# Fetching V of an attention block by one 1 MB DMA per step in place of two of 0.5 MB

## Chip, cores, metric

The kernel runs on one core of one Trainium2 chip. The metric is the device time of one execution in microseconds. Where two kernels are compared, they ran on the same chip in alternating rounds; the ratio is the mean time of one kernel's runs over that of the other's of the same rounds, so it is not quite the ratio of the medians that are quoted. A bracket after a ratio is its 95% interval. In the profiles PE is TensorE (PEld its weight loads), DVE is VectorE, ACT is ScalarE, POOL is GpSimd, and SP is SyncE, which here issues the DMAs.

## The reference

Two attention blocks with a cache of K and V, for 16 batches of 32 queries. A has 4 K/V heads shared by 32 query heads; B has 32 K/V heads of its own. The outputs are put side by side.

```python
# per block: x [16,32,1024], k_cache and v_cache [16,Hkv,1024,128], all bf16
q = (x @ wq).reshape(B, Sq, 32, 128).transpose(0, 2, 1, 3)
scores = einsum("bhqd,bhkd->bhqk", q, k) * 128 ** -0.5
o = einsum("bhqk,bhkd->bhqd", softmax(scores), v)
out = o.transpose(0, 2, 1, 3).reshape(B, Sq, 4096) @ wo
```

B's caches dominate the traffic: K and V of B are 128 MB (of 2^20 bytes) each.

## The kernel before

B is done in 128 steps. A step takes four heads of one batch: 1 MB of K and 1 MB of V. K has two slots in SBUF, V has three. A step of A runs beside each step of B.

```python
NVB_SLOTS = 3          # V of B
NKB_SLOTS = 2          # K of B
DMA_BW = 390e3         # what the scheduler believes of the DMA, bytes per us
SP_AHEAD = 1.5         # how far ahead of the DMA stream it lets SP issue, us

def st_dmaV(q):        # ... (the branch for B)
    sl = q.vslot
    for t_ in range(2):
        vsrc = pb["v"][q.b, q.h0 + 2 * t_:q.h0 + 2 * t_ + 2].rearrange("a (p c) d -> p a c d", c=NCH)
        pr.add("sp", lambda e, t_=t_, vsrc=vsrc: e.dma_start(VB_sb[:, sl, 2 * t_:2 * t_ + 2, :, :], vsrc),
               writes=[("VB", sl, t_)], dma_key=f"vb{sl}_{t_}", name="vb_dma", dur=2 * Sk * Dh * 2, ...)

# the value product of step q reads both halves
pr.add("pe", lambda e, c0=c0: e_pv(e, c0), reads=["PT", ("VB", kvs, 0), ("VB", kvs, 1)], writes=[BK_O], name="PVB", ...)
```

Nothing is issued in the order of these calls. Every operation is first put on a list with what it reads and writes and how long it should take. `list_schedule` then simulates all engines and the DMA stream, picks at each moment the ready operation with the longest way to the end, and so fixes the order of each engine's instructions. A DMA occupies the simulated stream for `dur / DMA_BW`:

```python
if op.dma_key is not None:
    free[op.eng] = st + 0.06
    xs = max(st + 0.06, dma_free[0])
    dma_free[0] = xs + op.dur / dma_bw
    op.t1 = dma_free[0] + dma_lat
# ...
seq = sorted(range(n), key=lambda k: (ops[order[k]].t0, k))     # the new order of the program
# ... in build():
pr = pr.list_schedule()
pr.finalize()                                                    # semaphores and waits
```

All DMAs go out on SP in the order of its program: a DMA that waits for its slot or its data holds all that stand behind it. The last additions of the output projection write a row block into one staging buffer, `ost`, from which an output DMA takes it. There are eight such blocks, and each has to leave before the next can be written.

## Time and profile before

| | before |
|---|---|
| time, median of the first 3 runs | 855.66 us (854.54 to 856.07) |
| span of the profiled run | 853.9 us |
| bytes moved, mean rate | 341.6 MB, 400 GB/s |

These lines are from the summary page of before: busy time per engine, the rate in 40 equal slices, the count of DMA packets, the share of 16 DMA engines' time that the SP queue's packets take, and for two kinds of DMA their count, size and median time from issue to landing.

```profile
PE 726.1 (85%) x12098; PEld 434.9 (51%) x12098; DVE 545.3 (64%) x1115; ACT 447.1 (52%) x981; POOL 67.9 (8%) x76
GB/s 353 395 411 400 412 405 409 413 410 377 407 406 405 416 411 412 410 401 415 409 409 411 410 412 406 413 410 414 413 401 411 397 410 413 414 411 411 412 385 158
DMA packets 126845, 341.59 MB, mean 400 GB/s; under 512 B 9984, under 2 KB 9984, under 8 KB 110336
q1 hardware_dynamic: 126720, 339.78, 100.7%
KB_sb<-in_B_k_cache_dram SPq DMA_DIRECT2D x128, 1024.0 KB, 8.9
VB_sb<-in_B_v_cache_dram SPq DMA_DIRECT2D x256, 512.0 KB, 10.1
```

The DMA stream is the bound: it is full from the first slices to the last but one, and no compute engine is. A 1 MB transfer lands 8.9 us after its issue because it queues behind others: at about 410 GB/s the megabyte itself is 2.6 us. The list of SP's own waits (who waited for whom: us in total, times, longest) shows that SP spends much of the span held by a buffer that isn't free yet, with that backlog in front of it:

```profile
SPq L784 <- DVE KBt_sb L819: 124.5, 36, 8.5
SPq L784 <- DVE stat L882: 100.9, 34, 5.9
SPq L791 <- POOL VAp_sb L793: 80.8, 28, 6.5
```

Line 784 issues K of B: it can go when DVE has done both transposes of the K that held the slot. When that slips, the backlog shrinks.

### The profile page before, as it was taken

Reading aid. Unit: us, or ns where it says so; the run is one execution under the profiler, and the core shown is the slowest. Engines: PE = TensorE matmul, PEld = TensorE weight load, DVE = VectorE, ACT = ScalarE, POOL = GpSimd, SP = SyncE. Lnnn points to the kernel's source line nnn. Section 1 sums busy time; section 2 is a strip of 40 time slices with the busy share of each in tenths; the row PEclk is TensorE's granted clock in tenths of the full one; section 3 lists DMA queues with packets and bytes.
Section 4 is the critical chain, followed back from the end, with each engine's and each line's share of the span. In section 5 each row is a group of like instructions: output and inputs, shape, how many; then the busy total and the mean of one; then the engine's idle time right before and its main releaser. Section 6 shows DMA issues by size and latency. Waiting matters only on the chain.

```text
span 853.9 us, 27413 instructions
## 1 busy us (share of the span) xinstructions
PE 726.1 (85%) x12098; PEld 434.9 (51%) x12098; DVE 545.3 (64%) x1115; ACT 447.1 (52%) x981; POOL 67.9 (8%) x76
## 2 busy tenths in 40 slices
PE   4999999789979897799997879887999867878885
PEld 2556655446545454455554445544555544545552
DVE  0755676567756677467774757675766755766673
ACT  2456666456645464445654445654565554556451
POOL 0000100100000000000000000000000000000000
PEclk9999999999999999999999999999999999999998
DMA  9999999999999999999999999999999999999994
GB/s 353 395 411 400 412 405 409 413 410 377 407 406 405 416 411 412 410 401 415 409 409 411 410 412 406 413 410 414 413 401 411 397 410 413 414 411 411 412 385 158
DMA packets 126845, 341.59 MB, mean 400 GB/s; under 512 B 9984, under 2 KB 9984, under 8 KB 110336
## 3 DMA queue, kind: packets, MB, share of 16 engines
q1 hardware_dynamic: 126720, 339.78, 100.7%
q8 instruction: 96, 1.57, 0.7%
q14 instruction: 29, 0.24, 0.1%
HBM read 337.64 MB, written 2.10 MB: 398 GB/s over the span
## 4 chain that ended last, share of the span: by engine, by line
DMA 49%; PE 29%; DVE 12%; SPq 5%; issue 3%; ACT 1%; POOL 0%; DVEq 0%; POOLq 0%
DMA KB_sb<-in_B_k_cache_dram 29%; DVE KBt_sb L819 10%; PE ps_pj L654 8%; PE ps_s L854 5%; DMA VB_sb<-in_B_v_cache_dram 5%; DMA KA_sb<-in_A_k_cache_dram 5%; PE ps_pj L708 4%; DMA VA_sb<-in_A_v_cache_dram 3%; PE ps_kt L912 3%; DMA wq_sb<-in_B_wq_dram 3%; PE ps_o L946 2%; SPq L799 2%; PE ps_pt L896 2%; PE ps_s L837 2%; DMA woB_sb<-in_B_wo_dram 1%
## 5 line engine op out<-in xcount | busy, mean ns | idle before, releaser
L819 DVE STREAM_TRANSPOSE KBt_sb<-KB_sb 128x1024 f32<-128x1024 f32 x256 | 306.2, 1226 | 75.8 <-DMA KB_sb<-in_B_k_cache_dram 67.8
L877 ACT ACTIVATE P_sb<-ps_s 128x512 bf16<-128x512 f32 x256 | 151.9, 599 | 88.3 <-PE ps_s L854 64.2
L869 ACT ACTIVATE PTA_sb<-ps_s 128x1024 bf16<-128x1024 f32 x128 | 131.3, 1026 | 89.8 <-PE ps_s L837 72.0
L854 PE MATMUL ps_s<-KBt_sb,QB_sb 32*32 32x512 bf16 x4096 | 144.4, 389 | 11.0 <-ACT P_sb L877 6.1
L584 ACT COPY PT_sb<-ps_pt 128x512 f32<-128x512 f32 x128 | 75.0, 586 | 122.3 <-PE ps_o L946 111.0
L654 PE MATMUL ps_pj<-xT_sb,wq_sb 128*128 128x512 bf16 x448 | 122.6, 392 | 10.7 <-DMA wq_sb<-in_B_wq_dram 3.7
L793 POOL COPY VAp_sb<-VA_sb 128x1024 bf16<-128x1024 bf16 x64 | 66.6, 1040 | 757.5 <-DMA VA_sb<-in_A_v_cache_dram 725.4
L946 PE MATMUL ps_o<-VB_sb,PT_sb 128*32 128x128 bf16 x4096 | 82.7, 223 | 35.4 <-DMA VB_sb<-in_B_v_cache_dram 21.2
L896 PE MATMUL ps_pt<-id,P_sb 128*128 128x128 f32 x512 | 99.2, 302 | 6.9 <-ACT P_sb L877 6.0
L946 PEld LDWEIGHTS ps_o<-VB_sb,PT_sb 128*32 128x32 bf16 x4096 | 61.2, 98 | 70.0 <-issue 66.1
L896 PEld LDWEIGHTS ps_pt<-id,P_sb 128*128 128x128 f32 x512 | 79.8, 206 | 27.3 <-ACT P_sb L877 9.6
L837 PE MATMUL ps_s<-QT_sb,KTA_sb 128*128 128x256 bf16 x512 | 83.1, 273 | 6.4 <-ACT PTA_sb L869 2.9
L912 PE MATMUL ps_kt<-VAp_sb,PTA_sb 128*128 128x129 bf16 x1024 | 77.8, 224 | 6.9 <-POOL VAp_sb L793 4.7
L854 PEld LDWEIGHTS ps_s<-KBt_sb,QB_sb 32*32 32x32 bf16 x4096 | 48.6, 89 | 65.7 <-issue 12.2
L962 DVE TENSOR_SCALAR OB_sb<-ps_o,rinv_all 128x128 bf16<-128x128 f32 x128 | 43.9, 343 | 59.4 <-PE ps_o L946 58.6
L912 PEld LDWEIGHTS ps_kt<-VAp_sb,PTA_sb 128*128 128x128 bf16 x1024 | 65.7, 99 | 31.6 <-POOL VAp_sb L793 14.0
L708 PE MATMUL ps_pj<-woB_sb,OTB_sb 128*128 128x512 bf16 x256 | 71.0, 384 | 10.0 <-DMA woB_sb<-in_B_wo_dram 3.8
L708 PE MATMUL ps_pj<-woA_sb,OTA_sb 128*128 128x512 bf16 x256 | 66.6, 385 | 7.9 <-DVE ost L724 3.5
L654 PEld LDWEIGHTS ps_pj<-xT_sb,wq_sb 128*128 128x128 bf16 x448 | 42.2, 109 | 45.9 <-DMA wq_sb<-in_B_wq_dram 6.3
L837 PEld LDWEIGHTS ps_s<-QT_sb,KTA_sb 128*128 128x128 bf16 x512 | 44.8, 98 | 30.4 <-ACT PTA_sb L869 7.1
L882 DVE TENSOR_TENSOR stat<-stat 64x1 f32<-64x1 f32 x256 | 41.9, 164 | 22.5 <-ACT P_sb L877 14.3
L721 DVE TENSOR_TENSOR acc<-acc,ps_pj 128x512 f32<-128x512 f32 x64 | 43.1, 674 | 20.4 <-PE ps_pj L708 19.1
(49 smaller groups left out, 504.8 us busy)
## 6 DMA issues: line engine op xcount, KB each, us to landing
KB_sb<-in_B_k_cache_dram SPq DMA_DIRECT2D x128, 1024.0 KB, 8.9
VB_sb<-in_B_v_cache_dram SPq DMA_DIRECT2D x256, 512.0 KB, 10.1
KA_sb<-in_A_k_cache_dram SPq DMA_DIRECT2D x64, 256.0 KB, 10.2
VA_sb<-in_A_v_cache_dram SPq DMA_DIRECT2D x64, 256.0 KB, 8.6
wq_sb<-in_B_wq_dram SPq DMA_DIRECT2D x16, 512.0 KB, 10.7
woB_sb<-in_B_wo_dram SPq DMA_DIRECT2D x32, 256.0 KB, 10.7
woA_sb<-in_A_wo_dram SPq DMA_DIRECT2D x32, 256.0 KB, 8.6
wq_sb<-in_A_wq_dram SPq DMA_DIRECT2D x12, 512.0 KB, 10.4
```

What stands on the lines that cost most here:

```text
L584: pr.add("act", lambda e: e.copy(dst_ap, src_ap), reads=reads, writes=writes, name=name + "@act", wtag=wtag, rtag=rtag)
L654: last = e.matmul(ps_pj[:, 0:NTOK], pick(src, j), xT_sb[:, pi, j, :], start=(j == 0), stop=(j == DJ - 1))
L708: last = e.matmul(ps_pj[:, 0:OUTW], OT[:, gp, hh, :], wo_[:, hh, oh * OUTW:(oh + 1) * OUTW], start=(hh == 0), stop=(hh == nh - 1))
L793: pr.add("pool", lambda g: g.tensor_copy(VAp_sb[:, sl, :, 0:Dh], VA_sb[:, :, :]), reads=["VA"], writes=[("VAp", sl)], name="VAp_cp", rtag= ...
L819: pr.add("dve", lambda e: e.transpose(KBt_sb[:, sl, t_, :].bitcast(F32).rearrange("p (s r i) -> p s r i", r=2, i=32), KB_sb[:, rs, t_, :]. ...
L837: last = e.matmul(ps_s[:, sbf, c2, i * 2 * P:(i + 1) * 2 * P], KTA_sb[:, sl, c * P:(c + 1) * P], qt, start=True, stop=True)
L854: last = e.matmul(ps_s[32 * cg:32 * cg + 32, sbf, g, :].rearrange("p (sh cl j) -> p sh cl j", sh=4, cl=4), lhsT, kt[32 * a:32 * a + 32, g, ...
L869: pr.add("act", lambda e: e.activation(dst, src, ACTF.Exp, scale=scale), writes=BK_S[sbf] + [("PTA", q.half)], name="expA", rtag={("Sv", s ...
L877: pr.add("act", lambda e, src=src, dst=dst, g=g: e.activation(dst, src, ACTF.Exp, scale=scale, accum_out=st[:, g:g + 1]), writes=[BK_S[sbf ...
L896: last = e.transpose(ps_pt32[:, m * P:(m + 1) * P], p32[:, m:Sk // 2:NPK], id32[:])
L912: last = e.matmul(ps_kt[:, qh * OA0:qh * OA0 + Dh + 1], PTA_sb[:, h, c, qh * P:(qh + 1) * P], VAp_sb[:, sl, 4 * h + c, 0:Dh + 1], start=(h ...
L946: last = e.matmul(ps_o[32 * a:32 * a + 32, 0:Dh], PT_pairs[:, c // 2, 32 * (a ^ (c // 4 * 2)):32 * (a ^ (c // 4 * 2)) + 32, c % 2], VB_sb[ ...
```

## The change

The intent is fewer, larger transfers: one DMA of 1 MB per step, one semaphore (the counter by which an engine learns that a transfer has landed), one wait. The diff is shortened at the dots.

```diff
-                for t_ in range(2):
-                    vsrc = pb["v"][q.b, q.h0 + 2 * t_:q.h0 + 2 * t_ + 2].rearrange("a (p c) d -> p a c d", c=NCH)
-                    pr.add("sp", lambda e, t_=t_, vsrc=vsrc: e.dma_start(VB_sb[:, sl, 2 * t_:2 * t_ + 2, :, :], vsrc), writes=[("VB", sl, t_)],
-                           dma_key=f"vb{sl}_{t_}", name="vb_dma", dur=2 * Sk * Dh * 2, wtag={("VB", sl, t_): q.kid})
+                vsrc = pb["v"][q.b, q.h0:q.h0 + 4].rearrange("a (p c) d -> p a c d", c=NCH)
+                pr.add("sp", lambda e: e.dma_start(VB_sb[:, sl, :, :, :], vsrc), writes=[("VB", sl)],
+                       dma_key=f"vb{sl}", name="vb_dma", dur=4 * Sk * Dh * 2, wtag={("VB", sl): q.kid})
...
-                pr.add("pe", ..., reads=["PT", ("VB", kvs, 0), ("VB", kvs, 1)], ...
+                pr.add("pe", ..., reads=["PT", ("VB", kvs)], ...
```

More of the change, by code (lines that the diff above doesn't have):

```diff
@@ L949, in st_pv @@
             for c0 in range(0, NCH, 2):
-                pr.add("pe", lambda e, c0=c0: e_pv(e, c0), reads=["PT", ("VB", kvs, 0), ("VB", kvs, 1)], writes=[BK_O], name="PVB",
-                       dur=0.116, tag="B%d" % q.t, rtag={"PT": q.qid, ("VB", kvs, 0): q.kid, ("VB", kvs, 1): q.kid}, wtag={"Ops": q.qid})
+                pr.add("pe", lambda e, c0=c0: e_pv(e, c0), reads=["PT", ("VB", kvs)], writes=[BK_O], name="PVB",
+                       dur=0.116, tag="B%d" % q.t, rtag={"PT": q.qid, ("VB", kvs): q.kid}, wtag={"Ops": q.qid})
         def st_recip(q):
```

## The prediction

> **What bounds the kernel now.** The DMA engines. The summary page gives 400 GB/s over the 853.9 us span; 34 of its 40 slices move 400 to 416 GB/s. Its queue table puts the SP queue's packets at 100.7% of 16 engines' time. TensorE is busy 85%, DVE 64%, ACT 52%. I also summed the issues and the packet records: between 20 and 830 us the bytes issued but not yet moved had a median of 2.6 MB and never fell under 0.3 MB. The engines always have a packet waiting, so time is bytes over rate, plus some 12 us of start and 15 us of drain.
>
> **What the change does.** V's bytes (128 MB), source runs (2 KB) and 65,536 data packets stay. There are 128 DMA instructions fewer (of 624) and 16 x 128 = 2,048 semaphore packets fewer (of 9,984, the "under 512 B" count). A 4-byte packet takes 9 ns in the records: 2,048 x 9 ns / 16 = 1.2 us goes away. A gap around each could add up to 1 us. Data packets keep their 84 ns per 2 KB (1st and 95th percentile alike).
>
> On SP the timeline shows 0.95 us for the two issues; one of twice the size should take 0.75 to 0.95 us. SP mostly waits (124.5 us on DVE's K transposes, by its list of waits) behind that backlog, so this is worth nothing. TensorE's value product read both halves already; its 21.2 us of waiting for V is off the critical path.
>
> The Trainium skill, "DMA: Bandwidth & Descriptors", section "Rules for kernel authors", asks for 1 MiB or more per DMA; its section "Bandwidth" rates single 1 MB transfers at 78% of peak. That promises a gain if transfers stand alone. Here they don't: the fixed cost hides under the backlog, and this mix of 0.25, 0.5 and 1 MB DMAs already streams at about 410 GB/s.
>
> **What moves.** The kernel orders its instructions by a list scheduler of its own, fed with each DMA's size. One entry in place of two reorders the SP queue and, through it, all engines. K of B can no longer slip between two halves of V. K has two slots; it lands 8.9 us after its issue (median), then come two transposes, 2.4 us: 11.3 us against two steps of 6.6 us (stream time / 128), about 2 us of slack; half a V is 1.3 us. Some backlog is lost, but it should not run dry. The end (last V issued at 831.3 us behind an output DMA, last instruction at 853.9) can shift a few us either way: the main spread.
>
> **Prediction.** 855.7 - 1.2 (semaphore packets) - up to 1 (gaps) + about 1 (coarser order) = 854.8 us; 8 in 10 within 850.5 to 860. Faster by over 2%: 0.01; within 2%: 0.96; slower by over 2%: 0.03.
>
> **What would show it.** Right: 496 issues, 7,936 packets under 512 B, data packets still 84 and 309 ns, slices still 400 to 416 GB/s, V's issue-to-landing 1 to 2 us above 10.1 us. Wrong: V packets slower; middle slices under 390 GB/s, or DVE waiting clearly more than 67.8 us for K (backlog ran dry); a tail 5 us longer or shorter.
>
> **What would make it wrong.** A reordered queue in which SP waits for a V or A slot with K behind it, so the stream starves each step; or four interleaved head streams in HBM running at another rate than two.

## The result

After took 859.69 us (median of 4 runs, 858.03 to 860.53) against 855.1 us for before (4 runs, 853.86 to 856.07). The ratio is 1.0051 [1.0035, 1.0068]: within 2% as forecast, and just inside the range, but the small effect has the opposite sign. I had expected to gain about 1 us; about 4 us were lost. That the time lies within the range is owed to the range's width. The same lines of the page of after:

```profile
PE 708.6 (83%) x11967; PEld 432.1 (50%) x12098; DVE 546.7 (64%) x1115; ACT 449.8 (52%) x981; POOL 67.9 (8%) x76
GB/s 342 387 406 389 412 411 409 410 415 406 407 408 409 409 410 400 412 414 399 407 399 412 411 411 416 392 409 415 405 413 413 407 404 411 415 412 411 409 373 108
DMA packets 124795, 341.56 MB, mean 398 GB/s; under 512 B 7936, under 2 KB 7936, under 8 KB 108288
q1 hardware_dynamic: 124672, 339.77, 100.3%
KB_sb<-in_B_k_cache_dram SPq DMA_DIRECT2D x128, 1024.0 KB, 9.0
VB_sb<-in_B_v_cache_dram SPq DMA_DIRECT2D x128, 1024.0 KB, 11.3
```

What was to be removed is removed: 128 issues, and 2,048 packets under 512 B. In the packet records the semaphore packets' time fell from 5.6 to 4.5 us per DMA engine. (PE's lower busy time comes with matmul records missing from the trace: 11,967 of 12,098.) The rest of the run looks much the same; the lowest slices are among the first four and the last two.

A view by windows says the same with less noise. Its columns are the window, its length, busy time and instruction count of PE, PEld, DVE, ACT and POOL, PE's clock, DMA share, and the rate in GB/s as the last number. First before, then after:

```profile
40.00:80.00 40.00, 39.16 (x498) 23.12 (x497) 21.23 (x46) 21.75 (x44) 3.13 (x3) 1.00 1.03 399
80.00:820.00 740.00, 638.77 (x10979) 385.12 (x10978) 490.96 (x1007) 403.45 (x892) 61.38 (x59) 0.98 1.03 409
```

```profile
40.00:80.00 40.00, 38.30 (x491) 23.37 (x498) 22.62 (x48) 21.61 (x43) 3.12 (x3) 1.00 1.01 384
80.00:820.00 740.00, 620.04 (x10853) 380.19 (x10965) 491.02 (x1005) 406.08 (x893) 60.79 (x59) 0.98 1.03 409
```

From 80 to 820 us both move 409 GB/s (a rounded figure: 1 GB/s more or less over 740 us would be 1.8 us). Between 40 and 80 us after moves 15 GB/s less, which is 0.6 MB, or 1.5 us of stream at 409 GB/s. From the packet records I took the time at which given amounts of data had been moved: after reached 26 MB 1.7 us later than before, needed 0.5 us less from there to 326 MB, 1.5 us more from 326 to 339 MB, and 2.0 us more from 339 MB to its end. That adds up to 4.7 of the 4.8 us between the two spans. In this pair of traces the loss is at the two ends. (One trace is one execution: five other traces with before's engine order reached 26 MB at 67.6 to 69.5 us, four others with after's at 68.5 to 70.6 us, so such a number scatters by about 2 us. The profiled execution of after, 860.53 us, was the slowest of its four.)

What goes on at the start can be read in the timelines (start, length, engine, line, operation, destination<-source, shape, count, and in brackets the idle time before and what ended it). Before, DVE and then SP:

```profile
46.45 2.37 DVE L819 STREAM_TRANSPOSE KBt_sb<-KB_sb 128x1024 f32<-128x1024 f32 x2 [0.36 <-DMA KB_sb<-in_B_k_cache_dram]
49.83 0.69 DVE L586 CAST QT_sb<-ps_pj 128x512 bf16<-128x512 f32 x1 [1.01 <-PE ps_pj L654]
...
48.85 0.33 SPq L784 DMA_DIRECT2D KB_sb<-in_B_k_cache_dram  x1
```

After, DVE and then SP:

```profile
47.31 1.25 DVE L818 STREAM_TRANSPOSE KBt_sb<-KB_sb 128x1024 f32<-128x1024 f32 x1 [1.69 <-DMA KB_sb<-in_B_k_cache_dram]
49.77 0.69 DVE L586 CAST QT_sb<-ps_pj 128x512 bf16<-128x512 f32 x1 [1.21 <-PE ps_pj L654]
...
51.64 1.25 DVE L818 STREAM_TRANSPOSE KBt_sb<-KB_sb 128x1024 f32<-128x1024 f32 x1
...
52.91 0.33 SPq L784 DMA_DIRECT2D KB_sb<-in_B_k_cache_dram  x1
```

Before does the two transposes of a K back to back, and SP issues the next K at 48.85 us. In after the scheduler put a copy of a projection between them. That copy waits for TensorE, more small work follows, and the second transpose only ends at 52.9 us. The next K goes out 4.1 us later, and V and the rest wait behind it on SP. This is a different order of DVE's instructions. No DMA has become slower.

That this late K costs the time is not shown, and finer windows speak against the simplest reading. First before, then after:

```profile
40.00:50.00 10.00, 9.69 (x123) 4.83 (x125) 5.76 (x14) 3.92 (x11) 1.05 (x1) 1.00 1.03 393
50.00:60.00 10.00, 9.91 (x147) 5.90 (x135) 6.51 (x12) 5.59 (x11) 0.28 (x1) 1.00 1.03 415
60.00:70.00 10.00, 10.00 (x140) 6.58 (x138) 6.27 (x14) 6.27 (x11) 1.80 (x2) 1.00 1.04 383
70.00:80.00 10.00, 9.56 (x109) 5.81 (x108) 2.69 (x8) 5.96 (x11) 0.00 (x0) 1.00 1.04 407
```

```profile
40.00:50.00 10.00, 9.79 (x133) 5.11 (x133) 6.01 (x14) 4.63 (x13) 1.04 (x1) 1.00 0.98 363
50.00:60.00 10.00, 9.45 (x147) 5.90 (x150) 5.61 (x12) 5.66 (x11) 0.00 (x0) 1.00 1.03 415
60.00:70.00 10.00, 9.77 (x133) 6.45 (x132) 8.14 (x16) 6.28 (x11) 2.08 (x2) 1.00 0.98 370
70.00:80.00 10.00, 9.30 (x86) 5.91 (x86) 2.87 (x7) 5.05 (x9) 0.00 (x0) 1.00 1.03 390
```

From 50 to 60 us, while the late K is held and just after, both move 415 GB/s out of the backlog. In the packet records nearly all of the dip of 40 to 50 us falls before 42 us, ahead of the split pair. The late K could only count later, between 60 and 80 us, where after moves 0.3 MB less; which wait makes that difference is open.

### The profile page after: what moved, and what is told of

It is laid out like the page before. It is cut to its first block, busy times and chain, and to the rows that moved or that the text cites. A ratio compares the mean times of both kernels' runs of the same rounds, so it can differ in the third digit from the quotient of the medians.

```text
span 858.7 us, 27077 instructions
## 1 busy us (share of the span) xinstructions
PE 708.6 (83%) x11967; PEld 432.1 (50%) x12098; DVE 546.7 (64%) x1115; ACT 449.8 (52%) x981; POOL 67.9 (8%) x76
## 2 busy tenths in 40 slices
DMA packets 124795, 341.56 MB, mean 398 GB/s; under 512 B 7936, under 2 KB 7936, under 8 KB 108288
## 4 chain that ended last, share of the span: by engine, by line
DMA 55%; PE 22%; DVE 15%; SPq 4%; issue 2%; ACT 1%; POOL 0%; DVEq 0%; POOLq 0%
DMA KB_sb<-in_B_k_cache_dram 32%; DVE KBt_sb L818 12%; DMA VB_sb<-in_B_v_cache_dram 10%; PE ps_pj L654 5%; PE ps_s L853 4%; PE ps_pj L708 4%; DMA wq_sb<-in_B_wq_dram 3%; DMA VA_sb<-in_A_v_cache_dram 2%; PE ps_o L945 2%; DMA KA_sb<-in_A_k_cache_dram 2%; DMA wq_sb<-in_A_wq_dram 2%; PE ps_kt L911 2%; DMA woB_sb<-in_B_wo_dram 2%; PE ps_pt L895 1%; PE ps_s L836 1%
## 5 line engine op out<-in xcount | busy, mean ns | idle before, releaser
L818 DVE STREAM_TRANSPOSE KBt_sb<-KB_sb 128x1024 f32<-128x1024 f32 x256 | 305.2, 1225 | 76.9 <-DMA KB_sb<-in_B_k_cache_dram 70.9
L654 PE MATMUL ps_pj<-xT_sb,wq_sb 128*128 128x512 bf16 x402 | 112.8, 390 | 15.2 <-DMA wq_sb<-in_B_wq_dram 4.5
L945 PE MATMUL ps_o<-VB_sb,PT_sb 128*32 128x128 bf16 x4096 | 81.6, 222 | 36.2 <-DMA VB_sb<-in_B_v_cache_dram 35.4
L945 PEld LDWEIGHTS ps_o<-VB_sb,PT_sb 128*32 128x32 bf16 x4096 | 59.1, 97 | 74.9 <-DMA VB_sb<-in_B_v_cache_dram 50.5
L836 PE MATMUL ps_s<-QT_sb,KTA_sb 128*128 128x256 bf16 x512 | 85.3, 275 | 8.5 <-ACT PTA_sb L868 5.1
L911 PE MATMUL ps_kt<-VAp_sb,PTA_sb 128*128 128x129 bf16 x1024 | 75.4, 222 | 7.6 <-POOL VAp_sb L793 6.0
L708 PE MATMUL ps_pj<-woB_sb,OTB_sb 128*128 128x512 bf16 x205 | 60.7, 390 | 13.8 <-DMA woB_sb<-in_B_wo_dram 4.7
L708 PE MATMUL ps_pj<-woA_sb,OTA_sb 128*128 128x512 bf16 x227 | 61.7, 391 | 10.6 <-DMA woA_sb<-in_A_wo_dram 4.0
## 6 DMA issues: line engine op xcount, KB each, us to landing
VB_sb<-in_B_v_cache_dram SPq DMA_DIRECT2D x128, 1024.0 KB, 11.3
```

The costliest lines, as they stand in the source:

```text
L654: last = e.matmul(ps_pj[:, 0:NTOK], pick(src, j), xT_sb[:, pi, j, :], start=(j == 0), stop=(j == DJ - 1))
L708: last = e.matmul(ps_pj[:, 0:OUTW], OT[:, gp, hh, :], wo_[:, hh, oh * OUTW:(oh + 1) * OUTW], start=(hh == 0), stop=(hh == nh - 1))
L818: pr.add("dve", lambda e: e.transpose(KBt_sb[:, sl, t_, :].bitcast(F32).rearrange("p (s r i) -> p s r i", r=2, i=32), KB_sb[:, rs, t_, :]. ...
L836: last = e.matmul(ps_s[:, sbf, c2, i * 2 * P:(i + 1) * 2 * P], KTA_sb[:, sl, c * P:(c + 1) * P], qt, start=True, stop=True)
L911: last = e.matmul(ps_kt[:, qh * OA0:qh * OA0 + Dh + 1], PTA_sb[:, h, c, qh * P:(qh + 1) * P], VAp_sb[:, sl, 4 * h + c, 0:Dh + 1], start=(h ...
L945: last = e.matmul(ps_o[32 * a:32 * a + 32, 0:Dh], PT_pairs[:, c // 2, 32 * (a ^ (c // 4 * 2)):32 * (a ^ (c // 4 * 2)) + 32, c % 2], VB_sb[ ...
```

## Experiments

Two theories stood against each other. **O**: the scheduler, fed one entry of 1 MB in place of two of 0.5 MB, arrives at another order of all engines' instructions, SP's included, and that order is what costs. **S**: the transfer of 1 MB itself costs, by its size or by its four head streams. Later came **L**: before's order is better than most that this scheduler makes, so nearly any disturbance costs some microseconds. All kernels gave correct results. The experiments were made in three groups of four, each beside 11 runs of before, whose medians were 855.15, 854.73 and 855.29 us. The diffs are shortened, some to a line of plain words.

### Before's order, merged V

After scheduling, the two halves are joined at the place of the second:

```diff
-        pr = pr.list_schedule()
+        pr = merge_halves(pr.list_schedule(), whole_v)   # drop the 1st half, emit VB_sb[:, sl] <- 4 heads at the 2nd
```

The instruction orders of TensorE, DVE, ACT and GpSimd were compared with before's: not one row differs.

> The scheduler is fed the two halves as before, so TensorE, DVE, ACT and GpSimd keep before's order instruction by instruction; after scheduling the two halves are sent as one 1 MB DMA at the place of the second. If the order made the 0.5% (theory O), this runs like before: 853 to 856 us, at best 1 to 2 us faster for its 2,048 missing semaphore packets. If the size of the DMA made it (theory S), it runs like after: 858 to 861 us.

Measured: 858.41 us (856.35 to 865.53, 6 runs), ratio 1.0067 [1.0034, 1.0101]. By its own expectation this spoke for S. But the edit isn't clean: in 19 of the 128 steps other transfers stand between the two halves, and there the first half is now fetched later. So the order on SP had changed too. Its trace doesn't lose between 40 and 80 us (406 GB/s); it moves 408 GB/s from 80 to 820 us where before moves 409, which is 0.7 MB or about 1.8 us. Which waits make that up I have not found.

### After's order, V split again

The scheduler is fed one 1 MB entry, as in after; then each V is emitted as two 0.5 MB DMAs back to back. The other engines' order is after's, row by row.

```diff
-        pr = pr.list_schedule()
+        pr = split_whole(pr.list_schedule(), halves_v)   # each vb_dma -> two of half the size, in place
```

> The reverse: the scheduler is fed one 1 MB entry as in after, so every engine has after's order; after scheduling each V is sent as two 0.5 MB DMAs back to back. Theory O: like after, 858 to 862 us (1 to 2 us above after at most, for the semaphore packets). Theory S: like before, 854 to 857 us.

Measured: 858.35 us (855.40 to 860.88, 6 runs), ratio 1.0049 [1.0033, 1.0065]. With the DMAs of before and the order of after, the whole loss is there. Theory O is shown to suffice. The two halves stand side by side in this run, as the whole V does in after, so it doesn't tell SP's order from that of the other engines. And its profiled execution was the fastest of the six, 855.40 us: its trace, used below, is of a run that lost next to nothing.

### Before's order, only adjacent halves merged

This is the clean form of the first run. Of the 128 pairs, 109 already stand side by side on SP; only these are joined, so no transfer changes its place.

```diff
+    joined = {x.tag for x, y in zip(sp, sp[1:]) if both are halves of the same V}
-        if name == "vb_dma":
+        if name == "vb_dma" and tag[0] in joined:
```

> Before's order on every engine, SP too: only the V pairs whose halves already stand side by side on SP are sent as one 1 MB DMA. No transfer changes its place. Theory O (the order alone): 853 to 856 us, 1 to 2 us faster at best. Theory S (a 1 MB V costs by its size, as the first run with before's order and merged halves suggests): 856 to 859 us.

Measured: 855.19 us (853.48 to 858.45, 6 runs), ratio 1.0011 [0.9987, 1.0036]. 85% of the change's merging costs nothing that could be measured, and gains nothing either. If size made the whole 0.5%, these 109 pairs should cost about 0.43% (an estimate, 0.85 of 0.51%), which is outside the interval: theory S falls as the account of the loss.

The two merges of before's order differ in the other 19 pairs alone: 1.0067 [1.0034, 1.0101] with them, 1.0011 [0.9987, 1.0036] without. The intervals just touch. All engines but SP keep before's order in both. So fetching V's first half later in 19 steps is enough to lose about what after loses; in before's SP rows it is a K that stands between the halves in 18 of the 19. The windows of this adjacent merge, and of after's order with halves, as above:

```profile
40.00:80.00 40.00, 38.92 (x493) 23.30 (x499) 21.19 (x46) 22.02 (x46) 3.12 (x3) 1.00 1.03 403
80.00:820.00 740.00, 623.65 (x10866) 381.79 (x10977) 490.50 (x1007) 402.99 (x892) 61.38 (x59) 0.98 1.03 409
```

```profile
40.00:80.00 40.00, 38.71 (x545) 23.80 (x540) 22.20 (x47) 23.09 (x45) 3.12 (x3) 1.00 1.01 394
80.00:820.00 740.00, 618.00 (x10840) 380.06 (x10944) 493.57 (x1005) 403.80 (x891) 61.40 (x59) 0.98 1.03 409
```

409 GB/s again in the body, whatever the size of V's DMAs. Between 40 and 80 us the rate of these single traces goes with the order: the six kernels with before's engine order show 397 to 406 GB/s (before, the two merges, the output on ACT, and the two with a second staging buffer below); the five with after's order show 378 to 394, whether V is whole or split. That is not yet the loss: the 394 is from the execution of 855.40 us.

### Other orders from the same scheduler

One constant that the scheduler believes is changed; nothing else. Each change shuffles the order from an early step on.

```diff
-DMA_BW = 390e3
+DMA_BW = 380e3        # in before, and in after
-SP_AHEAD = 1.5
+SP_AHEAD = 2.0        # in before
```

> Before with halves; only the DMA rate that its scheduler assumes is 380 in place of 390 GB/s, which shuffles the order of all engines. Theory L (before's order is a picked one, any other order of this scheduler costs some us, whatever the V size): 857 to 862 us. Theory V (orders made with halves are as good as each other, what costs is feeding the scheduler a 1 MB entry): 854 to 856 us.

Measured: 857.39 us (856.97 to 864.69, 6 runs), ratio 1.0050 [1.0018, 1.0081]: theory L's range.

> The same shuffle for after (whole V). Theory L: anywhere from 855 to 863 us, not systematically above the shuffled before. Theory V: 858 us or more.

Measured: 860.51 us (857.44 to 864.28, 6 runs), ratio 1.0070 [1.0043, 1.0098]: within both ranges.

> Before with halves, the scheduler's look-ahead of the DMA queue set to 2.0 in place of 1.5 us: a second shuffle. Theory L: 856 to 862 us, clearly above before. If before's order is nothing special: 853 to 857 us.

Measured: 856.70 us (855.88 to 857.61, 6 runs), ratio 1.0019 [1.0005, 1.0034]: again within both ranges.

Between 40 and 80 us the three move 382, 384 and 394 GB/s: all lie below before's 399, as after does. With halves kept, an unrelated constant costs 0.2% to 0.5%. So after's 0.5% is of the size that this scheduler's order varies by anyway (theory L). That before's order was picked by tuning these constants for two halves would explain it, but no run shows how they were found. Whether orders made with whole V are worse on average than orders made with halves stays open: two of each (1.0051 and 1.0070 against 1.0050 and 1.0019) are too few.

### The end: output DMAs from ACT

The last V stands on SP behind an output DMA whose data isn't ready. If that is what makes the end long, the output DMAs should leave SP.

```diff
+        new.add("act" if name == "out_dma" else eng, ...)    # after scheduling, in after and in before
```

> After, with its 8 output DMAs issued from ACT in place of SP, at the same place in the schedule, so that V and K no longer wait on SP behind an output whose data is not there yet. Theory O with the end as its main term: the tail after the last input shrinks, 854 to 857 us. If the last V is held by its slot and not by the output DMA in front of it: no change, 858 to 861 us.

Measured: 863.04 us (862.34 to 864.50, 5 runs), ratio to before 1.0096 [1.0081, 1.0110].

> The same edit to before. The last V waits behind an output DMA here too, about 4 us by the timeline: 851 to 854 us if the tail follows that wait, 854 to 856 us if not.

Measured: 864.07 us (861.65 to 865.59, 6 runs), ratio 1.0107 [1.0088, 1.0126].

Both expectations failed: it costs 4 us on after and 9 on before. DVE's waits after 760 us tell why, for before and for before with the output on ACT (the names are the waiting addition into the staging buffer and the DMA that empties it):

```profile
DVE ost L724 <- DMA out_dram<-ost: 4.7, 3, 2.4
```

```profile
DVE ost L731 <- DMA out_dram<-ost: 18.3, 7, 4.3
```

ACT's program holds what stands behind a wait, too. In the trace of before with the output on ACT, the third to fifth output DMA left 6.2, 7.0 and 2.5 us after their data was ready, because ACT stood before exponentials and copies that waited for TensorE; on SP those delays were 0.03, 3.1 and 0.03 us. The staging buffer stays full, DVE stops at its next addition, and K's transposes stand behind that on DVE.

### The end: last V ahead of the output DMA

```diff
+    specs.insert(o, specs.pop(v))     # after scheduling: the last vb_dma in front of the out_dma before it
```

> After, with one swap on SP: the last V is issued in front of the output DMA that stood before it (issued at 835.9 us, when DVE had the row ready; the slot of the last V came free about 833 us). If that head-of-line wait is the cost of the end: 2 to 3 us less than after, 856 to 858 us, and the last V issued about 833 us. If the end is bound by the additions behind the last V: as after, 858 to 861 us.

Measured: 863.64 us (863.04 to 866.73, 6 runs), ratio to before 1.0108 [1.0090, 1.0127]. The swap did what it should: the last V went out at 833.9 us. The expectation failed by the same route as before: the output DMA now queues behind a megabyte of V. The step of the chain of waits that is this DMA, then DVE's next addition, in after:

```profile
835.92 5.37 DMA out_dram<-ost
...
841.31 0.69 DVE L724 TENSOR_TENSOR ost<-acc,ps_pj 128x512 bf16<-128x512 f32 x1 [0.75 <-DMA out_dram<-ost]
```

and with the last V first:

```profile
836.59 7.92 DMA out_dram<-ost
...
844.53 0.69 DVE L738 TENSOR_TENSOR ost<-acc,ps_pj 128x512 bf16<-128x512 f32 x1 [3.03 <-DMA out_dram<-ost]
```

The DMA takes 2.55 us longer to land, and DVE waits 2.3 us longer, which is about half of what the swap cost (the medians lie 4.0 us apart). At the end the chain runs through the staging buffer, not through the last V.

### The end: a second staging buffer

If so, a second buffer should help. There is no room for another 2 KB per partition, so B's output uses a part of `xT_sb` that is dead by then; the order of all engines is held.

```diff
-                o_ap = ost[:, oh * OUTW:(oh + 1) * OUTW]
+                o_ap = xT_sb[:, 1, oh, :] if pi else ost[:, oh * OUTW:(oh + 1) * OUTW]
```

> After with its order held, but B's output rows staged in a second buffer (a part of xT that is dead by then), so that DVE's last additions needn't wait for the output DMA before. If the longer tail of after comes from that single buffer: 855 to 857 us. If from the last V's late issue on SP: no change, 858 to 861 us.

Measured: 856.88 us (855.14 to 861.42, 6 runs), ratio to before 1.0032 [1.0003, 1.0061]. In its trace 14.0 us pass from 339 MB to the end, against 16.6 us in after. That points the right way, but the interval overlaps after's, so a gain of about 2 us is suggested and not shown.

> Before, order held, with the second staging buffer for B's output. DVE waited 4.7 us for output DMAs near the end in before: 852 to 854 us if half or more of that comes off, 854 to 856 us if not.

Measured: 854.90 us (853.19 to 855.98, 6 runs), ratio 0.9994 [0.9979, 1.0009].

> Before's order, adjacent V pairs as one 1 MB DMA, and the second staging buffer: a candidate to beat both. 851 to 854 us if the fewer semaphore packets and the freer end add up; 854 to 857 us if neither is worth anything.

Measured: 855.78 us (855.05 to 856.19, 6 runs), ratio 1.0009 [0.9996, 1.0023]. On before's order the second buffer is worth nothing that could be measured, alone or with the 109 merged pairs. No version beat before. This last run also bounds the size effect: even with the second buffer, merged V in place is at most 0.23% above before and at most 0.04% below (both edits taken together, and for the 109 pairs only).

## Why the prediction was right or wrong

- **Bound by the DMA stream, within 2%**: right. From 80 to 820 us, 86% of the span, before and after both move 409 GB/s. The backlog didn't run dry: counted from both traces as in the prediction, it had a median of 2.6 MB in each, and 0.4 MB (before) and 0.2 MB (after) at the lowest, between 30 and 40 us. DVE waited 70.9 us for K in place of 67.8, and no slice but the first four and the last two is under 392 GB/s.
- **Counts, packet times, landing**: right. 7,936 small packets; medians of 84 and 309 ns for 2 and 8 KB in the records, as before; V lands after 11.3 us, 1.2 us above 10.1.
- **1.2 us saved on semaphore packets**: the packet time did go (5.6 to 4.5 us), but the clock shows no gain: the in-place merge drops 1,744 of the 2,048 packets and ran at 1.0011 [0.9987, 1.0036]. A gain of 0.1% is within that.
- **SP's issue would take 0.75 to 0.95 us**: wrong, without consequence. For V as a tile, the issue on SP (count, then ns: lowest, median, highest) was, in before and in after,

```profile
L799 SPq DMA_DIRECT2D VB_sb<-in_B_v_cache_dram x256: 367/469/3343, 15.9 to 831.8; - x128
```

```profile
L798 SPq DMA_DIRECT2D VB_sb<-in_B_v_cache_dram x128: 368/436/1983, 15.9 to 836.3; - x128
```

  so an issue of twice the bytes took no longer.
- **"About +1 (coarser order)"**: this is the step that failed, by its size. The term had the right sign, but a new order measured about +4 us (1.0049 with after's order and V still in halves). What I had reckoned into it, a K that can't slip between two halves, exists: taking that away in the 19 steps where transfers stood between, with all engines but SP held to before's order, ran at 1.0067 where the merge that leaves them alone ran at 1.0011. I had put it at half a V, 1.3 us, within the slack. The new order of DVE, TensorE and ACT I had named too, but reckoned nothing for it; an unrelated constant that reorders everything, with V in halves, cost 0.5% in one run and 0.2% in another. So SP's order alone can cost what after lost, and so can a new order with the halves kept; the runs don't say how after's 4 us divide between these.
- **"The end can shift a few us either way: the main spread"**: right. It shifted by about 3.5 of the 4.8 us between the two spans (1.5 us from 326 to 339 MB, 2.0 us after). How far these shares of one trace hold for the medians is not settled.
- **Waits for V on TensorE are off the critical path**: too strong. They grew (from 21.2 to 35.4 us for matmuls), of which the prediction said nothing, and in the page's chain of work that ended last, V's DMA has 10% of the span in after, 5% in before. The rate of the body did not move, so no cost of this is shown.
- **The skill's advice of 1 MiB or more**: the Trainium skill, "DMA: Bandwidth & Descriptors", sections "Rules for kernel authors" and "Bandwidth" (whose table is of DMAs issued from GpSimd, where these go out on SP), suggests a gain from 0.5 to 1 MB. These runs show none behind a backlog of 2.6 MB (median), as predicted.

## What to carry to other kernels

When a program goes through a scheduler, a change of one entry is two changes: the instruction itself, and a new order of everything. Separate them by fixing the order, making the edit after scheduling, and then the reverse; and shuffle the order by an unrelated constant to learn how many microseconds an order is worth before explaining any effect smaller than that. Merging transfers gained nothing here, behind a backlog of some 2.6 MB; no run shows what it does for a stream that runs dry between them.

## What the Trainium skill lacked or had wrong

- "DMA: Bandwidth & Descriptors", section "Rules for kernel authors": 1 MiB or more per DMA is given for full bandwidth. The page doesn't say that this fades when transfers are queued back to back: 0.5 MB and 1 MB transfers of V both gave 409 GB/s from 80 to 820 us, and the in-place merge ran at 1.0011 [0.9987, 1.0036].
- The same page, section "Issuing engines are not separate DMA queues", says that issuing from several engines only saves sequencer time. The section lacks the cost: the output DMAs issued from ACT took their place in ACT's program, left up to 7.0 us after their data in the third to fifth case, and the kernel took 1.0107 [1.0088, 1.0126] of before's time.
- The same page, section "Anatomy of one DMA", calls the cost of generating descriptors small and variable for the GpSimd path; it has no figure for how the issue of a DMA from SP grows with its size. Here the median issue on SP was 469 ns for 0.5 MB and 436 ns for 1 MB: doubling the bytes added nothing.
- The same page, section "Queues, rings and completion order", says that each DMA engine takes descriptors in ring order. It lacks what follows for an output DMA that a compute engine waits for: it landed after 5.37 us, and after 7.92 us with one more megabyte of V in front.
